# Softcap attention into a top-2 mixture of experts: re-taken score tiles, a later second pair, zeroing on GpSimd, and a new order

## The chip, the cores and the metric

The kernel runs on one core of one Trainium2 chip. The metric is the device time of one execution in microseconds (us); lower is better. The engines are PE (TensorE), ACT (ScalarE), DVE (VectorE), POOL (GpSimd) and SP (SyncE, which here only issues DMAs).

## What is computed

Eight batches, twelve heads, 448 positions, head size 64. First attention with a soft cap, then a layer of four attention experts of which a gate picks two for each position:

```python
scores = cap * np.tanh((scale * q @ k.T) / cap)        # per batch and head, cap = 30
x = softmax(scores) @ v                                 # (8, 12, 448, 64) -> (8, 448, 768)
topk = the 2 largest of x @ w_gate (4 experts)          # w: softmax over these two
for e in range(4):
    a = softmax(causal(scale * (x @ wq[e]) @ (x @ wk[e]).T))
    out += (w of e where e is in topk, else 0) * (a @ (x @ wv[e]) @ wo[e])
```

## The kernel before, in words

**Work and staging.** The first attention goes by pairs of heads: 48 pairs p, six to a batch. `load` (line 427) starts the DMAs of k, q and v for two pairs at a time (one at a time for pairs 0 and 1), nearly all on SP's queue; the last 64 rows of k and v come apart, as `ktf` and `vtf`, and of these the two k parts of pair 0 are issued by ACT's own queue. `setup_head` (462) clears the unused corners of the `ktf` and `vtf` buffers; in the kernel before DVE does that for the first buffer of each (the line of `zero`, 469) and GpSimd for the others. `setup_v` (477) writes the ones next to v. `cast` (585) turns k, q and v to f16, `tr` (617) transposes k (L633) and q (L623) through PE into `qk`.

`fill` (699) issues the scores of a pair: matmuls L687 for the two heads' three blocks of 128 keys, and L697 for the tails of both heads together. The scores of block 0 and the tails go to X, those of blocks 1 and 2 to Y, one after the other. `tanh` (731, line 738) reads X or Y on ACT, `expo` (line 749) takes the exp of a whole pair, `pv` (753, lines 764 and 771) multiplies with v, and `xt` divides and transposes into the rows of x, `xT`. Of the last batch, the six pairs handle 320 of the 448 query rows; the other 128 rows of all six follow as pairs 48 and 49 (three pairs of heads each; lines 836, 841, 850, 852, 858, 863).

The second layer of batch b runs beside the first attention of the batch behind it: projections (`b_v`, `b_qk`, 879 and 903), gate (`b_gate`), scores and their exp (`b_score`, L1025 and L1034), PV (L1083), scaling (`b_pv`, L1096 and L1098), transposes of oS into oT (L1116, L1124), output projection (`b_wo`, L1139) and store. For the last batch nothing is left to run beside it. `last` (1214) does its first 320 rows: projections of k and q (L1222), the gate (`gate_tail`, 1316, lines 1343 to 1356, tag 3, with one exp on ACT, L1347), v (L1251), masks and scores in two parts (L1265, L1275), exp into `pB` (L1285), PV (L1305) and `normed` (1164: reciprocal L1168, weights L1171, product L1176, transposes L1183, projection L1198). `last2` (1358) does its last 128 rows: kL, qL, v and gate (L1364, L1374), masks and scores (L1389, L1399), exp (L1406), PV (L1418). Line 346 is a helper's copy out of PSUM, on DVE or ACT, whichever the planner picks.

**PSUM.** Eight banks. X is one tile of three banks and Y one tile of two; A0, A1 and A2 are three tiles of one bank each:

```python
    X = psum.tile([128, 3, 512], f32, name="X")
    Y = psum.tile([128, 2, 512], f32, name="Y")
    BANK = {f"A{i}": psum.tile([128, 512], f32, name=f"A{i}") for i in range(3)}
    for i in range(3):
        BANK[f"X{i}"] = X[:, i, :]
```

So X0 to X2 and Y0, Y1 are slices of their tile. Once the scores of the first attention are through, the second layer's last steps use these slices as further banks (groups with the list `ANY`). Waits are kept by tile: a writer of one slice of X waits for the readers of another.

**The order.** No scheduler decides at build time; the kernel plans itself. Every step is registered in a graph (`Graph.op`, 56) with its engine, an occupancy, a latency and the keys that it reads and writes, from which its dependences come. The chain of ACT steps marked fixed (tanh, exp) sets a clock; `dues` (109) goes backward from it and gives each step the earliest time that one of its successors needs it, or, where it has no successor and no time of its own, INF:

```python
        for o in reversed(self.ops):
            d = INF
            ...
            for s, late in o.succ:
                d = min(d, s.due - self.gap(o, s, late) - (0.1 if s.eng != o.eng else 0.0))
```

`solve` (126) then lists the steps: at each turn, on the engine that is free first, of the steps that are ready it takes that with the smallest due time, with some corrections: a constant for steps inside a group, one for the steps marked first (scores, transposes), and a jitter from `SEEDS`, one seed for every 4 us of planned time. It also picks the bank of each group. The main loop (1442 to 1494) registers the pairs; at the end `for o in order: o.fn()` (1495 to 1497) emits the instructions in this order, and each engine runs its own in the order in which they were emitted.

**The queues.** SP issues its DMAs in that order, at most eight of the DMAs under way at a time: a ninth waits for one of those before it. ACT's queue holds its own DMAs among its other instructions, as they are listed.

Of the kernel before, what the change touches and what calls it, by code (L numbers as in the profile page):

```python
# [16 lines left out]
SWITCH = 0.1  # L17
WARM = 5.5
TAIL = 4
# [3 lines left out]
SEEDS = (0, 585, 0, 977, 539, 648, 93, 0, 288, 124, 0, 0, 300, 0, 93, 0, 0, 29, 195, 542, 0, 0, 882, 736, 232, 1, 811, 440, 0, 398, 415, 654, 0, 534, 605, 323, 676, 311, 261, 0, 543, 0, 689, 633, 0, 316, 873, 294, 810, 0, 812, 816, 0, 683, 401, 0, 975, 570, 626, 0, 0, 563, 664, 252, 0, 913, 135, 0, 0, 502, 824, 912, 0, 0, 0, 0, 0, 0)  # L23
# [22 lines left out]
class Graph:  # L46
# [79 lines left out]
    def solve(self, when, banks, lent):  # L126
# [45 lines left out]
        while len(order) < n:  # L172
            best = None
            for e, rs in ready.items():
# [8 lines left out]
                def rank(x):  # L183
# [3 lines left out]
                    d = u.due + lag if u.first or left < TAIL else max(u.due + lag, t0 + 0.751)  # L187
                    d -= 1.057 * (u.grp is not None and not u.opens and left >= TAIL)
# [5 lines left out]
                near = t0 + (0.0 if left >= TAIL else SWITCH + 0.02)  # L194
                t, o = min((x for x in c if x[0] <= near), key=rank)
                if e in ("PE", "DVE") and not o.first:
                    for t2, u in c:
                        if u.first and u.due + lag < t + o.occ + 0.505 and t2 < t + max(SWITCH + 0.01, min(o.occ, 0.25)):
                            t, o = t2, u
                            break  # L200
# [66 lines left out]
def kernel(  # L267
# [34 lines left out]
    psum = ctx.enter_context(tc.tile_pool(name="ps", bufs=1, space=bass.MemoryType.PSUM))  # L302
    ctx.enter_context(tc.manual_schedule())
# [6 lines left out]
    X = psum.tile([128, 3, 512], f32, name="X")  # L310
    Y = psum.tile([128, 2, 512], f32, name="Y")
# [8 lines left out]
    ANY = AUX + XB + YB  # L320

# [140 lines left out]
    def setup_head():  # L462
        dve(0.3, lambda: nc.vector.memset(warm, 0.0), w=["warm"], due=-9.0)
        gp(0.8, lambda: make_identity(nc, ident), w=["ident"])
        for i in range(NST):
            for nm, t in (("zk", ktf[i]), ("zv", vtf[i])):
                def zero(t=t, i=i):
                    for g in range(2):
                        (nc.vector if i < 1 else nc.gpsimd).memset(
                            t[64 * g : 64 * (g + 1), :, 1 - g], 0.0)  # L470

                if i < 1:
                    dve(0.35, zero, w=[(nm, i)], name="zero", due=-20.0 if nm == "zk" else None)
                else:
                    gp(0.4, zero, w=[(nm, i)], name="zero")
# [141 lines left out]
    def tr(p):  # L617
# [30 lines left out]
        pe(0, lambda: tk(g, (0, 1, 2)), kr, [("tps", p, "k"), ("qkw", t)], g, occ=0.165, name=f"trk{p}")  # L648
# [247 lines left out]
    def b_qk(b, ref):  # L896
        x = b % 2
        for r in range(2):
            for which in "kq":
                g = Group(AUX + XB, 2.4)  # L900
                w2 = (wq2 if which == "q" else wk2)[r]
                for j in range(NDC):
# [6 lines left out]
                        due=(ref, 10.562 + 3.575 * r + 1.8 * (which == "q")))  # L909
# [406 lines left out]
    def gate_tail(b, tag, g, ps, m, z, l, t, s_, key):  # L1316
# [21 lines left out]
        def d_(fn, r, w, n=1):  # L1338
            dve(0.07 + n * m / 960, fn, [(b, tag, y) if y != "v" else key for y in r],
# [191 lines left out]
```

## Time and profile before

| what | us |
|---|---|
| median of 3 runs (lowest, highest) | 321.96 (321.91, 322.67) |
| the execution that was profiled | 321.08 |
| its span, from the first to the last instruction | 319.4 |
| ACT busy in the span | 292.8 |
| PE busy in the span | 288.6 |
| DVE busy, POOL busy | 223.0, 178.8 |
| HBM read and written | 36.19 MB, 11.01 MB |

The profile is of one execution, so its own time stands beside its span: 1.68 us lie around the span. PE is the matmul array, PEld the loading of its weights, which overlaps; "idle before, releaser" is the time in which an engine waited ahead of an instruction, and the instruction that ended it. L and a number is a line of the kernel before.

### The profile page before, as it was taken

To read this page: it belongs to the slowest core of one execution; us is meant where nothing else is said; L and a number is where in the kernel's file an instruction comes from. 1 tells how busy PE (TensorE), PEld (TensorE's weight loads), DVE (VectorE), ACT (ScalarE), POOL (GpSimd) and SP (SyncE) were. 2 spreads that over 40 slices of the span, in tenths; PEclk is the share of its full clock that TensorE was granted. 3 is DMA by queue.
4 is the path that set the end of the run, shared out by engine and by line. 5 is a ranking of instruction groups with operands and counts; after the bars stand their busy time and mean duration, and the time that the engine had idled before them with its cause. 6 is when DMAs were issued, how large, how long until landed. Compare 5 with 4: busy or idle time off the path is not lost.

```text
span 319.4 us, 8956 instructions
## 1 busy us (share of the span) xinstructions
PE 288.6 (90%) x3483; PEld 194.9 (61%) x3483; DVE 223.0 (70%) x677; ACT 292.8 (92%) x248; POOL 178.8 (56%) x480
## 2 busy tenths in 40 slices
PE   7778699988999999999999999999999999988862
PEld 3454456676566765576656766686567765766541
DVE  3364566686669786887768876977679878757661
ACT  3999999999999999999999999999999999892642
POOL 7874338999429662977483764775368237012000
PEclk9985869999999999999999999999999999999999
DMA  6889997999995694377606681600005001300045
GB/s 179 237 211 260 250 289 205 273 259 250 244 274 182 185 253 102 104 197 220 176 9 227 174 247 33 207 26 2 2 0 175 2 4 55 120 2 2 1 174 173
DMA packets 65083, 47.79 MB, mean 150 GB/s; under 512 B 25744, under 2 KB 61328, under 8 KB 65040
## 3 DMA queue, kind: packets, MB, share of 16 engines
q1 hardware_dynamic: 64736, 46.98, 54.1%
q8 instruction: 27, 0.44, 0.6%
q10 hardware_dynamic: 304, 0.23, 0.2%
q14 instruction: 16, 0.13, 0.1%
HBM read 36.19 MB, written 11.01 MB: 148 GB/s over the span
## 4 chain that ended last, share of the span: by engine, by line
ACT 58%; PE 24%; DVE 6%; SPq 5%; DMA 3%; issue 3%; DVEq 0%; POOL 0%; ACTq 0%; POOLq 0%
ACT yp L738 28%; ACT yp L749 24%; ACT pB L1034 4%; PE A L903 3%; PE A L771 3%; PE Y L687 2%; SPq L443 2%; PE A L1139 2%; PE A L879 2%; DMA kf<-in_k_dram 2%; DMA qf<-in_q_dram 2%; PE X L1025 2%; SPq L552 1%; PE A L764 1%; PE A L1083 1%
## 5 line engine op out<-in xcount | busy, mean ns | idle before, releaser
L749 ACT ACTIVATE yp<-yp 128x3136 f16<-128x3136 f16 (+4 forms) x51 | 141.4, 2773 | 0.0
L738 ACT ACTIVATE yp<-Y 128x896 f16<-128x896 f32 (+2 forms) x100 | 99.7, 997 | 2.8 <-PE Y L687 2.7
L738 ACT ACTIVATE yp<-X 128x1344 f16<-128x1344 f32 (+2 forms) x50 | 67.6, 1353 | 0.1
L771 PE MATMUL A<-v,yp 128*128 128x65 f16 x1116 | 57.4, 197 | 0.0
L771 PEld LDWEIGHTS <-yp 128*128 128x128 f16 x1116 | 50.6, 100 | 3.9 <-issue 2.6
L764 PE MATMUL A<-vtz,yp 128*128 128x130 f16 x186 | 42.1, 227 | 4.7 <-ACT yp L749 3.2
L795 DVE TENSOR_TENSOR xk<-A,rca 128x256 f16<-128x256 f32 (+1 forms) x96 | 39.9, 415 | 2.8
L687 PE MATMUL Y<-qk 64*128 64x448 f16 (+2 forms) x216 | 36.7, 347 | 2.2 <-ACT yp L738 1.3
L609 POOL CAST v<-vf 128x384 f16<-128x384 f32 x48 | 24.6, 514 | 18.2 <-PE A L771 16.3
L653 DVE COPY qk<-A 128x960 f16<-128x960 f16 x47 | 29.6, 650 | 6.4 <-PE A L623 6.1
L590 POOL CAST k<-kf 128x384 f16<-128x384 f32 x47 | 23.7, 509 | 18.0 <-PE A L633 10.7
L593 POOL CAST q<-qf 112x512 f16<-112x512 f32 x44 | 27.0, 616 | 8.1 <-DMA qf<-in_q_dram 7.0
L346 DVE COPY ob<-A 128x384 f32<-128x384 f32 (+1 forms) x55 | 29.2, 553 | 2.1 <-PE A L1139 1.7
L1108 POOL TENSOR_TENSOR oS<-oB,oB 128x512 f16<-128x512 f16 x14 | 16.0, 1154 | 26.0 <-DVE oB L1098 10.4
L792 DVE RECIPROCAL rca<-A 128x4 f32<-128x4 f32 (+1 forms) x96 | 17.1, 178 | 17.1 <-PE A L771 15.7
L764 PEld LDWEIGHTS <-yp 128*128 128x128 f16 x186 | 18.4, 99 | 14.3 <-issue 7.4
L687 PEld LDWEIGHTS <-qk 64*128 64x128 f16 x324 | 14.1, 94 | 19.9 <-issue 13.7
L1098 DVE SCALAR_TENSOR_TENSOR oB<-A,rcb,mw 128x256 f16<-128x256 f32 x53 | 25.0, 481 | 1.6
L1139 PE MATMUL A<-wo,oT 128*128 128x384 f16 x112 | 24.4, 326 | 0.6 <-DVE qk L653 0.2
L1083 PE MATMUL A<-vB,pB 128*128 128x260 f16 x136 | 22.7, 275 | 1.7 <-DVE oB L1098 1.1
L879 PE MATMUL A<-wvg,xT 128*128 128x260 f16 x168 | 22.8, 274 | 0.0
L819 DVE COPY xT<-A 128x448 f16<-128x448 f16 (+1 forms) x48 | 18.1, 378 | 6.4 <-PE A L810 5.9
(211 smaller groups left out, 593.0 us busy)
## 6 DMA issues: line engine op xcount, KB each, us to landing
qf<-in_q_dram SPq DMA_DIRECT2D x23, 448.0 KB, 5.8
kf<-in_k_dram SPq DMA_DIRECT2D x23, 384.0 KB, 5.3
vf<-in_v_dram SPq DMA_DIRECT2D x23, 384.0 KB, 5.4
out_dram<-ob SPq DMA_DIRECT2D x23, 384.0 KB, 3.3
out_dram<-ob SPq DMA_DIRECT2D x9, 192.0 KB, 3.0
ktf<-in_k_dram SPq DMA_DIRECT2D x46, 32.0 KB, 4.5
vtf<-in_v_dram SPq DMA_DIRECT2D x46, 32.0 KB, 4.7
ob<-in_moe_wv_dram SPq DMA_DIRECT2D x2, 384.0 KB, 6.3
```

The lines of the kernel that those rows point to most:

```text
L346: (nc.scalar.copy if o.eng == "ACT" else nc.vector.tensor_copy)(dst(), src())
L593: e(q16[i], qf[s][:, h].rearrange("p h (c d) -> p c h d", c=QC))
L653: lambda: nc.vector.tensor_copy(qk[t], bank16(g)[:, 0 : S + 512]),
L687: nc.tensor.matmul(dst[:, g, o], t[r, S + 128 * (c + 1) : S + 128 * (c + 2)], t[r, qs], start=True, stop=True,)
L738: ACTS[what, p] = act(c_act(n * (b - a)), lambda: nc.scalar.activation(y[:, a:b, 0:n], src[:, 0 : b - a, 0:n], AF.Tanh, scale=isc / capf), ...
L749: act(c_act(n * (b - a), False), lambda a=a, b=b, n=n: nc.scalar.activation(y[:, a:b, 0:n], y[:, a:b, 0:n], AF.Exp, scale=capf), ks, ks, f ...
L764: nc.tensor.matmul(ps[:, n, :, :], y[:, 2, w : w + 128], vtz[u], start=(n == 0), stop=False, skip_group_check=True,)
L771: nc.tensor.matmul(ps[:, n, h, :], y[:, SLOT[c][h], w : w + 128], v16[u][:, h, c, :], start=False, stop=(c == 2), skip_group_check=True,)
L795: dve(c_dve(128 * m), lambda g=g, i=i, rc=rc, m=m: nc.vector.tensor_tensor(xk[p % NXK][:, 2 * i : 2 * i + m, :, :], view(g)[:, 0:m, :, 0:D ...
L879: nc.tensor.matmul(bank(g)[:, 0 : E * Dh + E], xT[x][:, j, w : w + 128], wvg[:, j, :], start=(j == 0), stop=(j == NDC - 1),)
L1083: nc.tensor.matmul(bank(g)[:, 0 : E * (Dh + 1)], pB[pi][:, o : o + 128], vB[x][:, c, :, :], start=(t == 0), stop=(t == len(cs) - 1),)
L1139: nc.tensor.matmul(bank(g)[:, 0 : D // 2], oT[x][r][:, w : w + 128], wo2[r][:, c0:c1], start=(r == 0), stop=(r == 1),)
```

## The change

- X and Y are taken from pools of their own. A new operation `apart` leaves such a pool and takes each of its banks again as a tile by itself; it is registered for X and for Y just ahead of `last`.
- Pair 1 is set up behind pair 0's X scores: its `setup_v`, `cast` and `tr` are registered after the tanh of X of pair 0, and its first transposes (`trk1`) wait for the key of pair 0's scores in X.
- All clearing of `ktf` and `vtf` is on GpSimd; the first (k, buffer 0) carries the early due time.
- Planner constants: new `SEEDS`; 0.751 to 0.726, 1.057 to 0.865, 0.0 to 0.003 and 0.505 to 0.527 in `solve`; 3.575 to 4.082 and 5.155 to 5.337 in due times; the small gate operations of the last batch get a latency of their occupancy plus 0.13. They give a new order on all engines.

```diff
 JIT = 1.12
-SEEDS = (0, 585, 0, 977, 539, 648, ...)
+SEEDS = (0, 585, 124, 977, 539, 0, ...)
 BEGIN = {"POOL": 0.8, "DVE": 0.9, "SP": 0.8, "ACT": 0.8, "PE": 1.25}
...
                         return -INF, 0.0, 0
-                    d = u.due + lag if u.first or left < TAIL else max(u.due + lag, t0 + 0.751)
-                    d -= 1.057 * (u.grp is not None and not u.opens and left >= TAIL)
+                    d = u.due + lag if u.first or left < TAIL else max(u.due + lag, t0 + 0.726)
+                    d -= 0.865 * (u.grp is not None and not u.opens and left >= TAIL)
                     k = SEEDS[int(t0 / 4.0)] if t0 < 4.0 * len(SEEDS) else 0
...
 
-                near = t0 + (0.0 if left >= TAIL else SWITCH + 0.02)
+                near = t0 + (0.003 if left >= TAIL else SWITCH + 0.02)
                 t, o = min((x for x in c if x[0] <= near), key=rank)
...
                     for t2, u in c:
-                        if u.first and u.due + lag < t + o.occ + 0.505 and t2 < t + max(SWITCH + 0.01, min(o.occ, 0.25)):
+                        if u.first and u.due + lag < t + o.occ + 0.527 and t2 < t + max(SWITCH + 0.01, min(o.occ, 0.25)):
                             t, o = t2, u
...
     psum = ctx.enter_context(tc.tile_pool(name="ps", bufs=1, space=bass.MemoryType.PSUM))
+
+    def score_pool(name, side):
+        p = tc.tile_pool(name=name, bufs=1, space=bass.MemoryType.PSUM, side=side,
+                         reuse_waits="tile")
+        return p, p.__enter__()
+
+    pools = {"X": score_pool("px", "left"), "Y": score_pool("py", "right")}
     ctx.enter_context(tc.manual_schedule())
...
 
-    X = psum.tile([128, 3, 512], f32, name="X")
-    Y = psum.tile([128, 2, 512], f32, name="Y")
+    X = pools["X"][1].tile([128, 3, 512], f32, name="X")
+    Y = pools["Y"][1].tile([128, 2, 512], f32, name="Y")
     BANK = {f"A{i}": psum.tile([128, 512], f32, name=f"A{i}") for i in range(3)}
...
     ANY = AUX + XB + YB
+
+    def apart(what, banks):
+
+        def fn():
+            pools[what][0].__exit__(None, None, None)
+            pools[what] = score_pool("p" + what + "1", "left" if what == "X" else "right")
+            for b in banks:
+                BANK[b] = pools[what][1].tile([128, 512], f32, name=b + "s")
+
+        G.op("PE", 0.0, fn, (), [("s", b) for b in banks], 0.0, name="apart", takes=banks,
+             frees=banks)
 
...
             for nm, t in (("zk", ktf[i]), ("zv", vtf[i])):
-                def zero(t=t, i=i):
+                def zero(t=t):
                     for g in range(2):
-                        (nc.vector if i < 1 else nc.gpsimd).memset(
-                            t[64 * g : 64 * (g + 1), :, 1 - g], 0.0)
-
-                if i < 1:
-                    dve(0.35, zero, w=[(nm, i)], name="zero", due=-20.0 if nm == "zk" else None)
-                else:
-                    gp(0.4, zero, w=[(nm, i)], name="zero")
+                        nc.gpsimd.memset(t[64 * g : 64 * (g + 1), :, 1 - g], 0.0)
+
+                gp(0.45, zero, w=[(nm, i)], name="zero", due=-20.0 if (nm, i) == ("zk", 0) else None)
 
...
         g = Group(AUX)
-        pe(0, lambda: tk(g, (0, 1, 2)), kr, [("tps", p, "k"), ("qkw", t)], g, occ=0.165, name=f"trk{p}")
+        pe(0, lambda: tk(g, (0, 1, 2)), kr + [("s", XB[0])] * (p == 1), [("tps", p, "k"), ("qkw", t)], g, occ=0.165, name=f"trk{p}")
         pe(0, lambda: (tq(g, 0, 2), tk(g, (-1,))), [("q16", i), "ident"] + ktr,
...
                         [(which, b, r)], g, name=f"{which}{b}_{r}",
-                        due=(ref, 10.562 + 3.575 * r + 1.8 * (which == "q")))
+                        due=(ref, 10.562 + 4.082 * r + 1.8 * (which == "q")))
                 dst = (qB if which == "q" else kB)[x][r]
...
         def d_(fn, r, w, n=1):
-            dve(0.07 + n * m / 960, fn, [(b, tag, y) if y != "v" else key for y in r],
-                [(b, tag, y) for y in w], g, name="g2")
+            c = 0.07 + n * m / 960
+            dve(c, fn, [(b, tag, y) if y != "v" else key for y in r], [(b, tag, y) for y in w],
+                g, name="g2", lat=c + 0.13)
 
...
             setup_b()
-        for x in (0, 1) if p == 0 else (p + 1,) if p < NP - 1 else ():
+        for x in (0,) if p == 0 else (p + 1,) if p < NP - 1 else ():
             if x % 2 == 0 and x >= 2:
...
                 pv(p - 1)
-                xt(p - 1, (ACTS["Y1", p], 5.155))
+                xt(p - 1, (ACTS["Y1", p], 5.337))
                 if p % HP == 0 and p < NP:
...
             tanh(p, what)
+            if p == 0 and what == "X":
+                setup_v(1)
+                cast(1)
+                tr(1)
     expo(NPV - 1, (("X", "Y1"), ("Y2",)))
     pv(NPV - 1)
+    apart("X", XB)
+    apart("Y", YB)
     last(fixed_last())
...
         o.fn()
+    for what in "YX":
+        pools[what][0].__exit__(None, None, None)
 # ---- launch: one core; inputs and outputs as the reference has them ----
```

More of the change, by code (lines that the diff above doesn't have):

```diff
@@ L22 @@
 JIT = 1.12
[L23 removed]
+SEEDS = (0, 585, 124, 977, 539, 0, 622, 413, 288, 124, 627, 249, 300, 0, 93, 705, 231, 725, 195, 693, 0, 0, 882, 0, 232, 295, 42, 256, 522, 398, 397, 654, 0, 933, 605, 112, 582, 311, 261, 0, 59, 0, 0, 633, 410, 316, 806, 294, 752, 0, 0, 599, 615, 0, 401, 1, 975, 570, 626, 0, 979, 481, 664, 252, 0, 913, 135, 0, 0, 0, 824, 0, 0, 0, 0, 0, 0, 0)
 BEGIN = {"POOL": 0.8, "DVE": 0.9, "SP": 0.8, "ACT": 0.8, "PE": 1.25}
```

## The prediction

> **What bounds the kernel now.** I read the page first: busy time of each engine, then the chain of work that ended last.
>
> ```profile
> PE 288.6 (90%) x3483; PEld 194.9 (61%) x3483; DVE 223.0 (70%) x677; ACT 292.8 (92%) x248; POOL 178.8 (56%) x480
> ...
> ACT 58%; PE 24%; DVE 6%; SPq 5%; DMA 3%; issue 3%; DVEq 0%; POOL 0%; ACTq 0%; POOLq 0%
> ```
>
> ACT leads, PE is close behind. A share over the whole span hides stages, so the table by stretches came next. Its columns are the stretch, its length, then busy us and instructions of PE, PEld, DVE, ACT, POOL, the granted PE clock, the DMA share and GB/s.
>
> ```profile
> 8.00:20.00 12.00, 9.28 (x115) 5.95 (x112) 5.45 (x14) 11.62 (x10) 9.66 (x46) 1.00 0.88 226
> 20.00:40.00 20.00, 14.34 (x155) 9.19 (x155) 10.39 (x32) 19.51 (x15) 10.28 (x28) 0.70 1.00 248
> 40.00:100.00 60.00, 56.46 (x678) 37.69 (x677) 41.64 (x120) 60.00 (x45) 42.94 (x111) 0.96 0.99 248
> ...
> 220.00:280.00 60.00, 58.81 (x735) 40.36 (x732) 47.21 (x146) 58.96 (x52) 27.19 (x65) 1.00 0.14 48
> ...
> 290.00:300.00 10.00, 8.78 (x96) 6.00 (x93) 6.93 (x28) 4.31 (x11) 2.29 (x2) 1.00 0.01 2
> 300.00:310.00 10.00, 7.35 (x89) 4.55 (x87) 6.30 (x21) 4.92 (x12) 0.00 (x0) 1.00 0.39 140
> ...
> ```
>
> Three stages, then. From 40 to about 278 ACT is never idle: only less ACT work, or a gap put into it, changes that stage. From 280 on, ACT is idle for a growing part, half of it in 290 to 310, and PE has waits: a tail of dependences. And a head up to 30, which the chain itself describes (start, us, what):
>
> ```profile
> 4.06 4.95 DMA qf<-in_q_dram
> ...
> 15.88 2.95 SPq L552
> ...
> 21.35 5.14 DMA kf<-in_k_dram
> ...
> 27.18 0.50 PE A L633 x3
> ...
> 28.99 0.51 PE Y L687 x2
> 29.52 0.92 ACT yp L738
> ```
>
> The reader is to see what is not in it: the first scores. The head's chain is the stream of loads on SP's queue, its issues and its waits, down to the load of k that pairs 6 and 7 need.
>
> **The change part by part.** The sum is made against the profiled execution: 321.08 us, of which the span is 319.4 and 1.68 lies around it. The median of the runs shown is 321.96, so 0.88 is added at the end.
>
> *1. The re-take: 0.* The new `apart` operation leaves the pool of X (then Y) and takes each bank again as a tile of its own. It writes only the keys of the score banks, and nothing behind it reads or writes those keys. So it has no successor; `dues` propagates times from successors, and it keeps the due time INF. `solve` takes the smallest due time, so it comes last on PE. In the order of the changed kernel the two re-takes stand at places 2762 and 2791 of 2795, behind the last user of those banks, and no instruction touches a tile made by them. X stays one tile of three banks and Y one of two, up to the end; a reader of one X bank still holds a writer of another. Cost and gain are nothing, except that the rest of the tail is ordered as if the banks were free.
>
> *2. Zeroing on GpSimd: 0.* These are the rows of the timeline that parts 2 and 3 use (start, us, engine, line, operation, idle time before it and what ended it):
>
> ```profile
> 0.78 1.19 ACTq L443 DMA_DIRECT2D ktf<-in_k_dram  x2
> ...
> 0.87 0.40 DVE L469 MEMSET ktf<- 64x128 f32 x2 [0.87 <-PEq L1512]
> ...
> 1.30 0.45 POOL L469 MEMSET ktf<- 64x128 f32 x2
> 1.39 0.27 DVE L463 MEMSET warm<- 128x256 uint32 x1
> ...
> 2.01 1.28 ACT L1438 ACT_TABLE_LOAD   x1 [2.01 <-issue]
> ...
> 4.69 1.31 SPq L443 DMA_DIRECT2D ktf<-in_k_dram  x2
> ...
> 6.00 0.51 POOL L590 CAST k<-kf 128x384 f16<-128x384 f32 x1 [0.19 <-DMA kf<-in_k_dram]
> ...
> 6.75 0.53 PE L633 MATMUL A<-ident,k 128*128 128x128 f16 x3
> ...
> 10.33 0.92 ACT L738 ACTIVATE yp<-Y 128x896 f16<-128x896 f32 x1 [0.28 <-PE Y L687]
> ...
> 29.52 0.92 ACT L738 ACTIVATE yp<-Y 128x896 f16<-128x896 f32 x1 [0.40 <-PE Y L687]
> ```
>
> DVE loses two pairs of memsets of 0.40; GpSimd gains two of 0.45 ahead of its first cast, at 6.00, which waits for a DMA by then anyway. Without that cover it would cost 0.9. The memset of `warm` is now DVE's first, 0.5 earlier, and so are the fills of PE; no work waits for those.
>
> *3. The head: +0.2.* Pair 1's three transposes (0.53 at 6.75) go behind pair 0's first scores. Those then start up to 0.5 earlier, and the tanh of Y at 10.33 loses its gap of 0.28: at the first few tanh, ACT is some 0.4 ahead. But that lead has to pass 29.52, where ACT waited 0.40 for scores that PE issued behind the transposes (27.18) of a k that landed at 26.49 (21.35 + 5.14). PE's order at that place is unchanged. So ACT's lead there becomes a longer wait, and only the landing counts.
>
> That landing moves the wrong way. The two DMAs that ACT's queue issued at 0.78 now stand behind the table load (1.28) and the warm-up activation, and so start about 1.5 later. The waits of SP's queue are renumbered by it: the second of the two loads in the row at 4.69, issued at about 5.35, waited for one of those two, and now waits for pair 1's k, which landed just before the cast at 6.00. It starts at about 5.9, and all of SP's loads behind it, except the k that is moved ahead of a v, are 0.4 to 0.55 later. What of this reaches 21.35? The DMA share is 0.88 in 8 to 20: 1.4 us of slack that can swallow it; and 1.00 in 20 to 40, where nothing is made up. Bounds: −0.4 (the landing earlier by as much, so that the wait of 0.40 goes) and +0.55 (the whole delay). I take +0.2, between nothing and the whole delay.
>
> A rule stands against this. The Trainium skill, "DMA: Bandwidth & Descriptors", section "Issuing engines are not separate DMA queues", says that a second issuing engine saves only sequencer time, which is usually small beside the transfer. By that rule the move costs 0 and the sum would be 0.2 lower. The chain disagrees here: SP's queue is a link of it.
>
> *4. The new order up to 278: +0.1.* New seeds and constants permute PE's other work between the scores. PE has 3.54 us free in the 60 us from 40 to 100 and 1.19 in those from 220. The columns that PE computes ahead of each score differ at most places by under 700, at a few by up to 2170, about 0.9 us. Scores are issued behind a tanh that frees their tile, so a late one opens a gap in ACT that nothing gives back. There are no gaps to remove, so the bounds are 0 and about 1; I take 0.1, near the no-gap rows.
>
> *5. The tail: +0.4.* Its rows:
>
> ```profile
> 285.52 1.84 ACT L749 ACTIVATE yp<-yp 128x1920 f16<-128x1920 f16 x1
> ...
> 288.70 0.21 ACT L1347 ACTIVATE gt<-gt 128x12 f32<-128x12 f32 x1 [1.34 <-DVE gt L1345]
> 288.82 0.82 ACT L749 ACTIVATE yp<-yp 128x768 f16<-128x768 f16 x1
> ...
> 293.34 0.43 ACT L346 CAST kB<-A 128x320 f16<-128x320 f32 x1 [3.70 <-PE A L1222]
> ...
> 294.16 0.46 DVE L346 CAST qB<-A 128x320 f16<-128x320 f32 x1
> ...
> 296.06 0.31 PE L1275 MATMUL X<-qB,kB 64*128 64x320 f16 x1
> ...
> 296.61 0.44 ACT L1285 ACTIVATE pB<-X 128x320 f16<-128x320 f32 x1 [0.40 <-PE X L1275]
> ...
> 298.62 0.15 DVE L1343 COPY gt<-A 128x4 f32<-128x4 f32 x1
> ...
> 299.51 0.17 DVE L1351 TENSOR_TENSOR gt<-A,tri 128x16 f32<-128x16 f32 x1
> ...
> 304.71 0.19 DVE L1168 RECIPROCAL X<-X 128x4 f32<-128x4 f32 x1 [0.27 <-ACT ob L346]
> ```
>
> Gain: the last exp (288.82) now comes ahead of the gate's exp (288.70), so it starts when the one before it ends, at about 287.3, 1.4 earlier. Through PV, the projections and the casts at 293.34 this is 1.3 us of lead.
>
> It is lost again to new waits inside the unsplit X. (a) The cast of v for the first scores (`vB`) now reads an X bank, on DVE, behind a cast of q (0.46) and gate operations; the masks and scores that PE writes into other X banks wait for it: about 296.5 in place of 296.06. (b) The first `pB` (296.61) now waits for transposes of oS that PE writes into X: about 297.25, +0.64, which contains (a). (c) The second scores' write into X waits for another cast of v that reads X (the before had it in an A bank): up to +0.7. Against (c), six of the gate's small DVE operations, which took from 298.62 to 299.68, are now ahead of oT, so the casts of v come up to 1.0 earlier; together −0.2. The sum at 304.71 is 0.64 − 0.2, so +0.4. From there on the order and the waits are those of before, so the end moves as much. Bounds: −0.9 (most of the lead kept) and +1.3 (b and c in full).
>
> **Sum:** 0.2 + 0.1 + 0.4 = +0.7 us: 321.78 on the profiled execution, 322.66 on the runs, so 322.7.
>
> **The rivals.**
> *A. Faster: the lead in the tail lives.* The mechanism is (b): the first `pB` against the oS transposes. If PE issues those before the `vB` cast is done, their end no longer counts, and the 1.3 us lead reaches the second scores less about 0.4 from (c). It decides at whether they end before about 295.3 (296.61 − 1.3). For it: 8.78 of 10 busy PE means work can be brought forward. Against it: oS itself comes from GpSimd after the last DVE products. Price −0.9 in the tail, −0.2 with a head at −0.1: 321.96 − 0.9, about 321.0.
> *B. Slower: a gap in the dense stage.* A score that arrives late behind reordered projections, three or four times by 0.5, or the loads later by more than 0.55: +1.5 to +2.6, so 323.5 to 324.6. It decides where PE's work ahead of a score passes ACT's tanh and exp before it. For: only 1.19 of 60 us free on PE. Against: the differences are mostly small.
> *C. The re-take works after all.* These are the longest waits of PE in the tail (engine, line, what it waited for: us, times, longest):
>
> ```profile
> PE X L1305 <- ACT yp L1406: 1.4, 1, 1.4
> PE X L1183 <- DVE oB L1176: 1.0, 1, 1.0
> PE X L1222 <- DVE xk L852: 0.5, 1, 0.5
> PE X L1418 <- ACT oTL L346: 0.5, 1, 0.5
> ```
>
> These write one bank of X while another engine reads a different one. Without them 3.4 us, less what else then is last: −2 to −3.4, about 319.
> The Trainium skill, "PSUM — Partial Sum Buffer", section "PSUM bank collisions raise a hardware error", asks for a semaphore guard by bank and quadrant only, so such waits need not be; that speaks for C's price, not for its coming true, as the tiles are unused.
>
> **How the numbers follow.** The forecast (parts 1 to 5, 321.6 to 324.0 as its own range: head −0.1 to +0.5, middle 0 to 0.4, tail −0.3 to +1.1) has 0.55; A 0.25; B 0.17; C 0.03. About 0.3%, 0.97 us, is what a measurement of this kernel can tell from no change. Faster than 321.0: some two thirds of A, all of C and a little of the forecast, 0.22. Slower than 322.9: nearly all of B and two fifths of the forecast, 0.39. The rest, 0.39, is the same. The range runs from 320.4 (A with its whole lead) to 324.6 (B).
>
> **What would show it right or wrong.** Right: no tile of single banks, and PE in the tail still waiting for readers of other X banks; the second tanh of Y without its gap of 0.28, and the wait near 29.5 as long or longer than 0.40; ACT at 60.00 in each stretch from 40 to 220; the last exp at about 287.3; the first `pB` of the tail not earlier than 296.6 plus the shift of the head. Wrong: that load of k issued before 21.3; a gap in ACT between 40 and 278; the reciprocal of the tail (304.71) earlier than in the before.

## The result, and the profile after

The changed kernel takes 324.87 us (median of four runs, 324.59 to 326.56) against 321.94 for the kernel before beside it (four runs, 321.12 to 322.67): 1.0103 times as long, with an interval of 1.0061 to 1.0145. It is slower by 2.9 us, where +0.7 was forecast, and 0.3 us beyond the end of the range. Medians and ranges, here and below, are of fast runs alone: a run more than 1.5% above the fastest of its kernel is left out.

The profiled execution took 325.00 us with a span of 323.3, so 3.9 more than the profiled one of before. The page of the changed kernel, busy time of the engines and the chain that ended last:

```profile
PE 290.0 (90%) x3483; PEld 196.0 (61%) x3483; DVE 223.5 (69%) x673; ACT 293.0 (91%) x248; POOL 178.5 (55%) x484
...
ACT 40%; PE 33%; DVE 8%; issue 6%; DMA 5%; POOL 4%; SPq 3%; DVEq 0%; ACTq 0%; POOLq 0%
```

The work is the same: ACT 0.2 more, PE 1.4 more. So it is mainly the waits that have grown. In the chain ACT fell from 58% to 40% and PE rose from 24% to 33%. The table by stretches of the changed kernel (columns as in the prediction) says where:

```profile
20.00:40.00 20.00, 14.95 (x159) 9.14 (x157) 11.60 (x33) 18.66 (x15) 9.20 (x30) 0.67 1.02 240
40.00:100.00 60.00, 56.18 (x665) 36.76 (x663) 40.44 (x119) 59.77 (x46) 42.92 (x111) 0.96 1.00 252
...
220.00:280.00 60.00, 58.81 (x738) 40.15 (x737) 46.74 (x146) 58.98 (x51) 27.96 (x67) 1.00 0.14 48
290.00:300.00 10.00, 7.00 (x72) 4.96 (x72) 6.35 (x28) 1.76 (x5) 2.28 (x2) 1.00 0.01 2
300.00:310.00 10.00, 7.90 (x80) 4.76 (x78) 5.36 (x18) 5.40 (x13) 0.00 (x0) 1.00 0.22 85
310.00:323.30 13.30, 4.69 (x52) 2.81 (x51) 4.81 (x15) 4.43 (x10) 0.00 (x0) 0.92 0.45 145
```

From 40 to 280 little moved. From 290 to 300 PE is busy for 7.00 of 10 us, where it had been for 8.78, and ACT for 1.76 in place of 4.31. The loss is in the tail.

To measure it, one needs a mark ahead of the tail that both kernels have. I take the start of a tanh of Y among the last pairs. First the row of the kernel before, then that of the changed kernel:

```profile
270.17 0.81 ACT L738 ACTIVATE yp<-Y 128x640 f16<-128x640 f32 x1
```

```profile
271.27 0.84 ACT L752 ACTIVATE yp<-Y 128x640 f16<-128x640 f32 x1
```

From this mark to the end of the span are 319.4 − 270.17 = 49.23 us before and 323.3 − 271.27 = 52.03 after. The tail is 2.80 longer, and the mark 1.10 later. In what follows, "tail" is this length. It repeats within 0.5 us from kernel to kernel with the same order in the tail, mostly within 0.2, while the position of the mark scatters by some us.

These are the rows of the tail (timeline of the changed kernel) that stand for the ones that the prediction quoted:

```profile
286.64 2.58 ACT L763 ACTIVATE yp<-yp 128x1920 f16<-128x1920 f16 x2
...
296.68 0.42 ACT L364 CAST kB<-A 128x320 f16<-128x320 f32 x1 [0.72 <-PE A L1236]
...
297.62 0.46 DVE L364 CAST qB<-A 128x320 f16<-128x320 f32 x1
...
298.96 0.43 DVE L364 CAST vB<-X 128x256 f16<-128x256 f32 x1 [0.31 <-PE X L1279]
...
299.44 0.29 PE L1289 MATMUL X<-qB,kB 64*128 64x320 f16 x1 [0.59 <-DVE vB L364]
...
300.32 0.44 ACT L1299 ACTIVATE pB<-X 128x320 f16<-128x320 f32 x1 [0.62 <-PE X L1130]
...
305.63 0.44 ACT L1299 ACTIVATE pB<-X 128x320 f16<-128x320 f32 x1 [2.67 <-PE X L1289]
...
308.58 0.19 DVE L1182 RECIPROCAL X<-X 128x4 f32<-128x4 f32 x1 [0.26 <-ACT ob L364]
```

The projections of `last` give two casts of k and two of q, one of each for experts 0 and 1 and one for experts 2 and 3. The `kB` cast that the prediction quoted (293.34, from an A bank) and the one above (296.68) are those of experts 2 and 3. The first scores are those of experts 0 and 1. Before, the last cast that they need is that of the other k, on DVE; in the changed kernel it is the cast of q at 297.62. The row of the kernel before:

```profile
295.14 0.48 DVE L346 CAST kB<-X 128x320 f16<-128x320 f32 x1
```

With the 1.10 of the mark taken off each:

| step | before | after | difference − 1.10 |
|---|---|---|---|
| last exp ends | 289.64 | 289.22 | −1.52 |
| `kB` cast of experts 2 and 3 starts | 293.34 | 296.68 | +2.24 |
| last cast for the first scores ends | 295.62 | 298.08 | +1.36 |
| first scores of `last` in X | 296.06 | 299.44 | +2.28 |
| first `pB` | 296.61 | 300.32 | +2.61 |
| `pB` of the second part | 301.31 | 305.63 | +3.22 |
| first reciprocal of the end | 304.71 | 308.58 | +2.77 |
| end of the span | 319.4 | 323.3 | +2.80 |

The last two exps are one piece now, and the lead of 1.5 is there. Then 2.9 us are lost up to the last cast for the first scores (3.8 up to the `kB` of experts 2 and 3), and 0.9 more from there to the first scores: DVE's cast `vB` waits for masks that PE writes into other banks of X (L1279, 0.31), and then PE waits for `vB` (0.59). Behind the first scores 0.5 is added. The instructions of the first and larger piece, from the timeline of the changed kernel:

```profile
289.41 0.22 PE L850 MATMUL X<-vtz,yp 128*128 128x130 f16 x1
...
291.61 0.38 PE L1097 MATMUL X<-vB,pB 128*128 128x260 f16 x2 [0.19 <-DVE rc L864]
...
292.03 0.56 DVE L866 TENSOR_TENSOR xk<-X,rc 128x384 f16<-128x384 f32 x1 [0.48 <-PE X L1097]
292.64 0.30 PE L1236 MATMUL X<-xT,wq 128*128 128x320 f16 x1 [0.51 <-DVE xk L866]
...
292.97 0.17 DVE L1110 RECIPROCAL rcb<-X 128x1 f32<-128x1 f32 x1 [0.39 <-PE X L1236]
...
293.56 0.48 DVE L1112 SCALAR_TENSOR_TENSOR oB<-X,rcb,mw 128x256 f16<-128x256 f32 x1 [0.35 <-PE X L872]
294.10 0.30 PE L1236 MATMUL X<-xT,wq 128*128 128x320 f16 x1 [0.58 <-DVE oB L1112]
...
294.43 0.36 DVE L877 COPY xT<-X 128x384 f16<-128x384 f16 x1 [0.39 <-PE X L1236]
...
294.84 0.30 PE L1236 MATMUL X<-xT,wq 128*128 128x320 f16 x1 [0.18 <-DVE xT L877]
```

Read the releasers from row to row: PE waits for DVE, DVE for PE, PE for DVE. The PV of pair 49 (L850) was put into a slice of X. Another slice holds the projection of q for `last` (L1236, wq), a third the PV of the batch before (L1097), and the transposes of xk (L872) go into X as well. All are one tile, so a matmul into any slice waits for the DVE read of any other, and a DVE read waits for the matmul issued last. The eight waits in these rows, of both engines, sum to 3.07 us.

### The profile page after: what moved, and what is told of

Its sections match the earlier page's. It is cut to its first block, busy times and chain, and to the rows that moved or that the text cites. A ratio compares the mean times of both kernels' runs of the same rounds, so it can differ in the third digit from the quotient of the medians.

```text
span 323.3 us, 8962 instructions
## 1 busy us (share of the span) xinstructions
PE 290.0 (90%) x3483; PEld 196.0 (61%) x3483; DVE 223.5 (69%) x673; ACT 293.0 (91%) x248; POOL 178.5 (55%) x484
## 4 chain that ended last, share of the span: by engine, by line
ACT 40%; PE 33%; DVE 8%; issue 6%; DMA 5%; POOL 4%; SPq 3%; DVEq 0%; ACTq 0%; POOLq 0%
ACT yp L752 19%; ACT yp L763 16%; PE A L917 4%; PE A L785 4%; ACT pB L1048 4%; PE Y L701 3%; PE A L893 3%; PE A L1153 2%; PE X L1039 2%; SPq L461 2%; DMA qf<-in_q_dram 2%; PE A L778 2%; PE A L1097 2%; DVE ob L364 2%; DMA vf<-in_v_dram 1%
## 5 line engine op out<-in xcount | busy, mean ns | idle before, releaser
L893 PE MATMUL A<-wvg,xT 128*128 128x260 f16 x168 | 23.5, 274 | 0.0
L637 PE MATMUL A<-ident,q 112*128 112x112 f16 x192 | 22.3, 220 | 0.5 <-POOL q L607 0.5
```

Of the source, the lines that this page charges most:

```text
L893: nc.tensor.matmul(bank(g)[:, 0 : E * Dh + E], xT[x][:, j, w : w + 128], wvg[:, j, :], start=(j == 0), stop=(j == NDC - 1),)
```

## Experiments

Each kernel is named as in its heading; "tail" and "mark" are as above. The kernel before ran beside each of them, and the ratios are to it.

### The re-take made to work

The theory after the result: the two re-takes come too late to split anything. Then a due time should change that. `e1_retake_in_place` is the changed kernel with

```diff
-    def apart(what, banks):
+    def apart(what, banks, due):
...
-        G.op("PE", 0.0, fn, (), [("s", b) for b in banks], 0.0, name="apart", takes=banks,
-             frees=banks)
+        G.op("PE", 0.0, fn, (), [("s", b) for b in banks], 0.0, due, name="apart",
+             takes=banks, frees=banks)
...
-    apart("X", XB)
-    apart("Y", YB)
+    apart("X", XB, (ACTS["X", NPV - 1], 4.0))
+    apart("Y", YB, (ACTS["Y2", NPV - 1], 4.0))
```

> The changed kernel, with a due time for the re-take of X and Y (4 us after the last tanh that reads them), so that it is emitted ahead of the last batch's second layer and the single-bank tiles are really used. Up to PE's row 6503 the order is that of the changed kernel. Theory 1 (the re-take came too late; the 2.8 us lost in the tail are waits inside the unsplit X and Y, which the new order did not count on): the tail loses its waits for readers of other banks and gets 3 to 5 us shorter than the changed kernel's, 320 to 322 us. Theory 2 (the new order is itself worse in the tail, by its own dependences, whichever tiles it uses): 324 to 325.5 us, within 0.7 of the changed kernel. Either way the first 278 us stay 1.1 us later than in the kernel before.

`e2_retake_alone` is the kernel before with the pools and this `apart`, and nothing else of the change.

> The kernel before, plus only the pools of their own and the re-take with the same due time; all of its order up to the tail is unchanged. Theory 1: waits for other banks are 3 us or more of its tail too, so 318 to 320 us. Theory 2: the tail is held by dependences and not by the tiles, so 321 to 322.5 us.

Measured: e1 315.25 us (0.9811, 0.9762 to 0.9860), tail 42.13; e2 313.87 (0.9771, 0.9721 to 0.9821), tail 42.11. Both are below the range of either theory. The stretch 290 to 300 of e1, and below it the longest waits of PE from 272 on in e1:

```profile
290.00:300.00 10.00, 9.95 (x108) 7.06 (x106) 8.08 (x35) 3.69 (x11) 2.26 (x2) 1.00 0.01 2
```

```profile
PE A L872 <- DVE xk L866: 0.5, 1, 0.5
PE X L701 <- ACT pB L1048: 0.3, 1, 0.3
```

PE is full, and the waits of X for the readers of other banks are gone. The PV of pair 49 is still in a bank of X, but that bank is a tile by itself now (X0s):

```profile
288.85 0.22 PE L850 MATMUL X0s<-vtz,yp 128*128 128x130 f16 x1
```

On the order of before, the split takes 7.1 us off the tail (49.23 to 42.11), on that of the changed kernel 9.9 (52.03 to 42.13); what the two orders differed by in the tail is gone with the waits. The Trainium skill, "PSUM — Partial Sum Buffer", section "PSUM bank collisions raise a hardware error", asks for a guard by bank and quadrant only; these runs agree, as 7.1 us of waits that went beyond it could go.

### Which part made the changed kernel slower

`e3_head_steps_alone` is the changed kernel without `apart` and with the seeds, constants and gate latency of before. `e4_no_retake` is the changed kernel less two lines:

```diff
-    apart("X", XB)
-    apart("Y", YB)
```

> The changed kernel without the re-take and with the planner constants, seeds and gate latencies of the kernel before: only the later second pair and the zeroing on GpSimd are left. Theory 1 for the head (the 1.25 us gap of ACT near 24 comes from the new seeds, which put the load and the cast of wv ahead of a copy of xT on DVE): here xT is ahead of that cast, so the gap is under 0.5 and the time is 321.8 to 322.5 us, the tail that of the kernel before. Rival (the gap comes from the later second pair or the zeroing): the gap of about 1.2 is there, and the time is 322.6 to 323.3 us.

> The changed kernel without the two re-take operations, everything else kept. Theory 1 (as emitted, last, they do nothing): the order differs only in the tail, and the time is within 0.7 us of the changed kernel, 324.2 to 325.6 us. Rival (standing in the plan, they keep short-lived groups out of the banks of X and Y to the end, and this is what costs the tail): 322 to 323.2 us, with the tail about as long as in the kernel before.

Measured: e3 323.00 (1.0042, 1.0001 to 1.0084), so the steps of the head seem to cost something by themselves, though the interval only just leaves 1 out; its profiled execution took 327.08, so the gap of ACT near 24 that the expectation turns on is not read from it. e4 is at 321.79 (1.0009, 0.9971 to 1.0047), tail 48.69. So the 2.9 us came back in e4, within the interval, when two operations were removed that split nothing. My theory that they are inert fell. In e4, the PV of pair 49 is in a bank of its own:

```profile
291.90 0.22 PE L850 MATMUL A<-vtz,yp 128*128 128x130 f16 x1
```

How can a dead operation do that? Two ways were open: it does something when the pool is left, or its mere presence draws another order. In `solve`, the jitter of a step is computed from its number, `(u.idx * 40503 + k * 9973) % 1009`, and two operations more shift the number of each step registered behind them. `e5_two_empty` is e4 with

```diff
+    for b in ("X0", "Y0"):
+        G.op("PE", 0.0, lambda: None, (("s", b),), (), 0.0)
```

so it has no pool left and no tile taken. `e6_pv49_in_A` is the changed kernel with the PV of pair 49 kept out of X and Y:

```diff
-        g, gt = Group(ANY, 2.0), Group(ANY, 1.0)
+        ab = AUX if p == NP + 1 else ANY
+        g, gt = Group(ab, 2.0), Group(ab, 1.0)
```

> The kernel of e4 (no re-take), with two empty operations on PE in the place of the two re-takes: they take no bank and emit nothing. The order that comes out is the changed kernel's, instruction by instruction. Theory 1 (the dead re-take acts only by moving the numbers of the operations behind it by two, on which the jitter of the plan hangs, and so draws another order for the tail): 324.2 to 325.6 us, as the changed kernel. Rival (leaving the pools, or the banks reserved for the re-take, cost the 3 us): 321.2 to 322.6 us, as e4.

> The changed kernel, with the PV of the last pair and its transposes kept to the banks A0 to A2 (in the changed kernel they are in X, beside projections and PVs of the second layer that are in other banks of X). Up to the first of these instructions the order is the changed kernel's. Theory 1 (the loss in the tail is made between the last exp and the first casts of k and q, by PE and DVE waiting in turn for each other inside X, about 3 us of waits in seven pieces): 1.5 to 3 us shorter, 321.9 to 323.4 us. Rival (it is made later, at the first and the second pB, by the copies of v and of oS that are in X): 324.2 us or more.

Measured: e5 326.71 (1.0159, 1.0107 to 1.0210), tail 52.21; e6 323.95 (1.0058, 1.0022 to 1.0095), tail 48.93. The empty operations give the very order of the changed kernel on all engines, and its tail. With the PV of pair 49 kept out of X, the whole loss of the tail is gone, 3.1 us: the rows of e6 where PE computes the last third of pair 49 and ACT casts k,

```profile
294.09 0.22 PE L851 MATMUL A<-vtz,yp 128*128 128x130 f16 x1
...
294.77 0.38 PE L1098 MATMUL X<-vB,pB 128*128 128x260 f16 x2 [0.28 <-DVE oB L1113]
...
296.50 0.43 ACT L364 CAST kB<-A 128x320 f16<-128x320 f32 x1
```

have `kB` of experts 2 and 3 22.43 us behind the mark (274.07 in e6), against 25.41 in the changed kernel and 23.17 before. By the last cast for the first scores, 2.0 of the 3.1 are gained, and by the first scores 3.0. The edit is not as small as it looks: behind that PV the planner drew the order anew, and the v projections ahead of the first scores, their cast `vB` and the transposes of oS went from X to A banks with it. The median of e6 is only 0.9 below that of the changed kernel and lies between the ranges of its two theories, since its mark was 2.8 later; that is the stage of the loads, below.

`e16_tail_without_jitter` leaves the two dead operations in and sets the seeds from 276 us of planned time on to 0; of these only one, for 280 to 284 us, was not 0 already. (What its expectation calls a tanh of X is the mark, a tanh of Y.)

> The changed kernel, its re-take dead as there, with all seeds from 276 us on at zero, so that no jitter acts on the tail. If the changed kernel's tail (52.0 us from the tanh of X at 270.2 in the kernel before to the end) is one bad draw among many, this one lies elsewhere, 48 to 50.5 us, and the time at 321.5 to 324 us. If the loss hangs on the new constants and gate latencies, it stays at 51.5 to 52.5 us, and the time at 324 us or more.

Measured: 322.35 (0.9998, 0.9965 to 1.0032), tail 48.83. In e16 the PV of pair 49 is in Y, while the cast of v just ahead of the first scores still reads X:

```profile
291.91 0.22 PE L850 MATMUL Y<-vtz,yp 128*128 128x130 f16 x1
...
299.05 0.43 DVE L364 CAST vB<-X 128x256 f16<-128x256 f32 x1 [0.24 <-PE X L1279]
```

Three ways out of that one draw (e4, e6, e16) give 48.7 to 48.9, and two ways into it (the changed kernel, e5) 52.0 to 52.2. The bad tail is one draw of the jitter. The three good tails have the PV of pair 49 outside X, in A, A and Y; the two bad ones have it in X, undivided. That this place is what costs rests on these five, on e1, where it is in an X bank that is a tile by itself, and on the rows of waits; no run moves it and leaves all else as it was.

### The head

The stage of the loads was to be judged with the tail short, where less else moves. `e7_head_and_retake` is e2 with both steps of the head (zeroing on GpSimd, later second pair) and the planner's constants of before; `e8_retake_alone_again` is e2 once more, measured together with e7.

> The changed kernel with the constants, seeds and gate latencies of the kernel before and with the re-take in its place (due time as in e1); so e2 plus the later second pair and the zeroing on GpSimd. Theory 1 for the head (the two steps delay the loads by some tenths and gain nothing): 0.3 to 1.0 us above e8, 314.2 to 315. Rival (they cost nothing, or the first tanh being earlier pays): within 0.3 us of e8 or below it.

> The same kernel as e2, again, beside e7 on the same chip: the kernel before with the re-take in its place. 313.2 to 314.6 us by every theory.

Measured: e7 316.24 (0.9813, 0.9767 to 0.9859), e8 313.63 (0.9749, 0.9700 to 0.9797); both tails 42.1. So the steps of the head cost 2.6 us by the medians and 2.1 by the ratios, more than either theory had, and all of it ahead of the mark, though the runs of the two just overlap (314.47 to 317.08 and 313.10 to 314.93). Four kernels measured together take them apart:

- `e9_zeroing_alone`: e8 and only the zeroing on GpSimd (with it, ACT's two DMAs fall behind the table load)
- `e10_second_pair_alone`: e8 and only the later second pair
- `e11_both_dmas_first`: e7 with those two DMAs ahead of the table load again, by `r=[(z, s)] if e == "SP" else []`
- `e12_retake_alone_third`: e8, for the comparison

> e8 (the kernel before with the re-take in its place) plus the zeroing on GpSimd alone. In its order ACT's two ktf DMAs stand behind the table load, as in the changed kernel. Theory 1 for the head (this is what costs: the loads of SP's queue are later by it and the stage in which the DMA engines are full, up to 110 us, never makes it up): 1 to 2.5 us above e12, 315 to 316.8 us. Rival 1 (the later second pair costs): within 0.4 of e12. Rival 2 (neither; the load stage differs from run to run by as much): all four kernels within 0.8 us.

> e8 plus the later second pair alone; ACT's DMAs stand first, as in the kernel before. Theory 1: within 0.4 us of e12. Rival 1: 1 to 2.5 us above e12, and e9 is not.

> e7 (both head steps and the re-take in its place), with ACT's two ktf DMAs no longer planned behind the zeroing (they write other parts of the buffer), so that they are issued ahead of the table load again. Theory 1: it gets e7's loss back and is within 0.5 us of e12, and the second of the two next ktf loads on SP's queue starts at about 5.4 and not 5.5 to 5.9. Rival 1: it stays 1 to 2.5 us above e12.

> The same kernel as e2 and e8, beside e9 to e11 on the same chip: 313.2 to 314.6 us by every theory.

Measured: e12 314.08 (313.25 to 314.97, six runs), e9 315.51 (315.09 to 316.64), e10 315.89 (315.36 to 318.06), e11 318.44 (315.87 to 320.19). Each step alone costs 1.4 to 1.8 us; not one of the runs of e9 or e10 is as fast as the slowest of e12. So the number of theory 1 came true for e9 and not for e10. The two costs together make 3.2, where both steps in one kernel (e7) cost 2.6. The place of ACT's DMAs is not what costs in e9: they start at 1.22 there and at 0.79 in e12, but SP's loads behind them are not late by it, and the load of k for pairs 6 and 7 is issued at 20.53 in e9 and at 20.87 in e12. e11 fits that, as it gained nothing, but it is no clean test: its plan has another order on PE and DVE, and its tail is 43.57, 1.4 longer than that of e7.

What else do the two steps do? In e9 there is a long wait to follow back. DVE's timeline there, then that of e11 at the same instruction (in e12 it takes 0.87):

```profile
65.95 1.62 DVE L987 TENSOR_SCALAR g_w<-g_e 128x4 f32<-128x4 f32 x1 [0.83 <-POOL g_e L979]
67.61 0.18 DVE L988 RECIPROCAL g_w<-g_w 128x4 f32<-128x4 f32 x1
67.70 0.63 DVE L666 COPY qk<-A 128x960 f16<-128x960 f16 x1
```

```profile
64.41 0.31 DVE L987 TENSOR_SCALAR g_w<-g_e 128x4 f32<-128x4 f32 x1
```

A small gate operation of batch 0 waits on DVE for GpSimd and then runs long; the copy of transposed q and k behind it starts 6.0 us after the tanh of X ahead of it (61.68), where in e12 it is 4.4 (65.13 after 60.77), and with it the scores are late. ACT's timeline of e9:

```profile
70.21 0.92 ACT L751 ACTIVATE yp<-Y 128x896 f16<-128x896 f32 x1 [1.59 <-PE Y L700]
```

Three kernels, again measured together, take the two gate operations of batch 0 off DVE. The edit

```diff
-        dve(0.11, lambda: V.tensor_scalar_add(w0, e, 1.0), [(b, "e")], [(b, "w0")], lat=0.17)
-        dve(0.1, lambda: V.reciprocal(w0, w0), [(b, "w0")], [(b, "w0")], lat=0.18)
+        if b == 0:
+            g_(b, lambda: nc.gpsimd.tensor_scalar(w0, e, 1.0, None, ALU.add), ...)
+            g_(b, lambda: nc.gpsimd.tensor_tensor(w0, w0, min1[:, w], ALU.pow), ...)
```

is made in e9 (`e13_zeroing_gate_off_dve`), in e1 (`e14_changed_gate_off_dve`) and in e8 (`e15_retake_gate_off_dve`).

> e9 (re-take in place, zeroing on GpSimd) with batch 0's two gate operations that wait on DVE for GpSimd's g_e (add 1, reciprocal) done on GpSimd itself (add, then a power of -1); PE's order is the same but for one instruction group. Theory 3 (DVE, in order, is held up at g_w by a late GpSimd chain, and this makes ACT's gap of 1.6 us near 70): the gap goes to under 0.4 and the time is 1 to 1.6 us below e9, 313.9 to 314.6 us. Rival (the loads themselves are late, and the gap would only move): within 0.5 us of e9.

> e1 (the changed kernel with the re-take in its place) with the same edit. In e1 DVE waits 1.64 us at g_w, and ACT has gaps of 0.95 and 1.27 at 66 to 69 us. Theory 3: both gaps go to under 0.4, and the time is 1.2 to 2.2 us below e1, 313 to 314.1 us. Rival: within 0.5 us of e1's 315.25.

> e8 (the kernel before with the re-take in its place) with the same edit, as a control: DVE does not wait at g_w there, so both theories expect no gain, 313.3 to 314.8 us; a small loss is possible, as the edit puts some 1 us on GpSimd.

Measured: e13 314.62 (312.94 to 315.60, four runs), e14 315.11 (314.70 to 315.69, five runs), e15 313.40 (0.9733, 0.9693 to 0.9772). The gaps of ACT at 66 to 70 us, which e9 and e1 had, are gone in e13 and e14. But e14 is as long as e1 (315.25), where theory 3 had 313 to 314.1. ACT's timeline of e14 has other waits, at places where e1 had none:

```profile
17.98 0.92 ACT L753 ACTIVATE yp<-Y 128x896 f16<-128x896 f32 x1 [0.92 <-PE Y L702]
...
30.14 0.92 ACT L753 ACTIVATE yp<-Y 128x896 f16<-128x896 f32 x1 [1.05 <-PE Y L702]
```

And e13, at the upper end of theory 3's range, is 0.9 below e9; but the control e15 is 0.7 below e12 too, and e13 stays 1.2 above e15, as e9 stays 1.4 above e12. So that wait is real and removable, but it is at most a small part of what the steps of the head cost. What the rest is stays open. e15 is the fastest kernel of the study, 8.1 us under the kernel before beside it (321.52).

How firm is any number of this stage? Up to the tail, the changed kernel, e1, e4, e5, e6 and e16 have the same instructions in the same order on every engine. Their marks in the profiled executions stand between 271.27 and 274.07. Before, e2, e8 and e12 share the other order, and theirs stand between 269.28 (e8) and 270.99 (e2). By medians less the tail's difference, the order of the changed kernel costs +0.1 (its own runs), 0.9 (e1), 0.9 (e4), 1.2 (e16), 2.2 (e5) and 2.7 us (e6) ahead of the mark; the order of before in e2, e8 and e12 −0.8 to +0.1. So the new order is later there, by 1.3 in the mean, and one comparison of it is worth no more than ±1.3. Kernels measured together agree better (e1 and e4 0.9 each, e5 and e6 2.2 and 2.7). The waits themselves move: from 9 us to the mark, ACT's sum to 1.44 us in the changed kernel, 2.22 in e1, 2.99 in e5, 3.16 in e4, 4.12 in e16 and 4.82 in e6, at other places each time. A wait of this stage that is read from one execution, as in e9 above, need not be there in the next.

## Why the prediction was wrong, step by step

**The cause: part 5, "Through PV, the projections and the casts at 293.34 this is 1.3 us of lead."** The lead existed (last exp −1.52 against the mark). What failed is the passage through PV, projections and casts: the text took over the 3.70 us from the last exp to `kB` from the kernel before, though in the new order PV of pair 49, which had been in Y (L836 into Y from 289.49 on), stands in X among projections and other PVs. It took 7.46 (289.22 to 296.68), 3.8 more. To the last cast for the first scores it took 8.86 (289.22 to 298.08) where it had been 5.98 (289.64 to 295.62), 2.9 more: in place of a lead of 1.3 there is a lag of 1.36. With that PV outside X (e4, e6, e16), or in an X bank that is a tile by itself (e1), no such loss is there. The text looked for waits inside X only from the `vB` cast on: (a), (b) and (c). These three it had about right. From its lead to the first `pB` it gave (a) and (b) 1.94 (−1.3 to +0.64); they took 1.25 (+1.36 to +2.61). (c) came to +0.61 of "up to +0.7" at the second `pB`, and +0.16 was left of it at the reciprocal, where −0.2 was given. So of the error of 2.4 in this part (+2.77 for +0.4), the passage ahead of (a) makes 2.7, and the rest nearly cancels.

**Part 1, the re-take: 0.** That no tile of a single bank is used was right, and so was PE's waiting for readers of other banks. "Cost and gain are nothing" was wrong: e4 and e5 show that the dead operations turn a tail of 48.7 into one of 52.0 by shifting the numbers that go into the jitter, and e16 that without the jitter the loss is gone. The prediction had the resulting order in hand and counted it under part 5, so this was no error of the sum, but it named no such cause and priced it nowhere.

**Part 2, zeroing: 0.** Wrong by about 1.4 us in e9 against e12. Where these 1.4 are made is not shown; they lie ahead of the mark, as the tails are alike (42.17 and 42.07). Whether the cover that was named, GpSimd waiting for a DMA, held was not tested by itself.

**Part 3, the head: +0.2.** Right in its first half: the gap of 0.28 at the second tanh of Y is gone. The rest was wrong in the mechanism, and the later second pair, for which +0.2 was given, costs 1.8 by e10 against e12. These rows are from the head's timeline of the changed kernel:

```profile
10.01 0.92 ACT L752 ACTIVATE yp<-Y 128x896 f16<-128x896 f32 x1
...
20.51 1.23 SPq L457 DMA_DIRECT2D kf<-in_k_dram  x1
21.06 1.00 DVE L568 CAST wvg<-ob 128x384 f16<-128x384 f32 x1
...
22.40 0.27 PE L778 MATMUL A<-vtz,yp 128*128 128x130 f16 x1 [0.60 <-DVE xT L833]
...
24.41 0.92 ACT L752 ACTIVATE yp<-Y 128x896 f16<-128x896 f32 x1 [1.25 <-PE Y L701]
...
30.11 0.92 ACT L752 ACTIVATE yp<-Y 128x896 f16<-128x896 f32 x1
```

The load of k was issued at 20.51, before 21.3 and not after it: the prediction's own sign that this step is wrong. The wait at 29.52 is gone, and one of 1.25 stands at 24.41, behind a cast of weights on DVE ahead of PE's work. Yet e1, with the same instructions, had no wait there and two (0.95, 1.27) at 66 to 69. The story of ACT's DMAs was mis-sized at its first step. The rows of the changed kernel, and below them the one of before for its last:

```profile
0.78 1.28 ACT L1453 ACT_TABLE_LOAD   x1 [0.78 <-PEq L1535]
1.22 1.20 ACTq L461 DMA_DIRECT2D ktf<-in_k_dram  x2
...
6.16 0.60 SPq L461 DMA_DIRECT2D vtf<-in_v_dram  x1
```

```profile
6.04 0.60 SPq L443 DMA_DIRECT2D vtf<-in_v_dram  x1
```

The two DMAs start 0.44 later (1.22 for 0.78), not 1.5, since the table load itself moved up from 2.01 to 0.78; and SP's loads behind are 0.12 later, not 0.4 to 0.55. The Trainium skill, "DMA: Bandwidth & Descriptors", section "Issuing engines are not separate DMA queues", which the prediction set against its +0.2, calls the sequencer time saved by a second issuing engine usually small; these 0.12 us agree with it.

**Part 4, the order up to 278: +0.1.** ACT is busy for 59.77 of the 60 us from 40 to 100, where it was for 60.00, so a gap was put in, one of the prediction's signs of being wrong, if a small one (0.23 us); within the bounds of 0 to 1. Together, parts 2 to 4 were given +0.3. The runs of the changed kernel itself say +0.1, its profile +1.1, and the six kernels with its order +1.3 in the mean.

**The rivals.** A died ahead of the place that (b) names, where the lead was gone already; there `pB` still waited for the transposes of oS in X (0.62). B had nearly the right size (2.6 at most) in the wrong stage. C had the right mechanism for a working re-take (e1, e2) with half its price: it added up four rows, 3.4 us, of a list that goes on, and it counted only PE's share of waits in which PE and DVE take turns. The tail lost 7.1.

**The range** ended at 324.6, with rival B; the forecast itself ended at 324.0, as the tail's bound, +1.3, came from waits (b) and (c) alone, and the tail took +2.80. An estimate from the same trace was at hand: each further group in X may add a wait of about 0.5 (the L1222 row quoted there) on PE.

## What to carry to other kernels

Where waits are kept by tile and a tile spans several banks, follow each group that moves into it through the whole stretch from its last input to its first reader, on both engines; a place in the tile can cost more than the sum of the waits listed for one engine. An operation that does nothing can still move the time if an order is drawn with its number, so compare orders, not intentions, and give such a step a due time if it is to act. And measure a tail from a mark shared by both kernels: here tails of one order repeat within 0.5 us, where the mark itself moves by up to 2.8. An edit that makes a planner draw anew (e6, e11) changes more than it names, so look at what else moved before a cause is named.

## What the runs showed of the hardware that was not expected

The same DVE operation on 128x4 numbers (add 1 of batch 0's gate) took 1.62 us in e9, 0.92 in e2, 0.87 in e12 and 0.31 in e11. GpSimd ran casts beside it without a pause, in e11 too. The last of five in a row in e9, from its timeline:

```profile
67.04 0.51 POOL L603 CAST k<-kf 128x384 f16<-128x384 f32 x1
```

It ended at 67.55, the DVE operation at 67.57. In e2 and e12, too, the operation ended 0.02 and 0.01 us behind a cast with which GpSimd's row of casts stopped (66.17 and 66.15, 65.00 and 64.99); in e11 it ended at 64.72, with the cast before it on GpSimd at 64.70, while the next one ran. The Trainium skill, "SBUF — State Buffer", section "SBUF: two separate sides", says that DVE and GpSimd share a pair of ports as an exclusive lock: for a DVE operation in a two-port mode or with two inputs from SBUF, whichever starts first has it for its whole instruction, and the other blocks fully. These rows agree with it as far as the ends go together. It is argued as the cause and not shown: no run here takes the port away, none tells whether this operation is of that kind, and a lock held for one instruction does not say why five casts went ahead of it in e9.

The same stream of instructions reached the mark at times up to 2.8 us apart in different executions (271.27 and 274.07), with the DMA share at about 1.0 from 20 to 100 us. Past that stage, tails of the same order differ by 0.2 at most (42.07 to 42.17 in e2, e8, e9 and e12), but for e13 and e15, which end 0.4 to 0.5 sooner (41.68 and 41.64) with the same order on PE, DVE and ACT in the tail; why is open.
